# Two weight loads ahead of chunk 16, a choice that reads PSUM, and counts in front of the early products

## The chip, the cores and the metric

One core of one Trainium2 chip runs the whole program once. The time is device microseconds of that core, from the start of the program to its end; lower is better. Five engines work at once, each through its own instruction list in order: TensorE (PE in the profile; its weight loads are PEld), VectorE (DVE), ScalarE (ACT), GpSimd (POOL) and SyncE (SP, which issues most of the transfers). An instruction starts when it is the next one on its engine and the semaphores it waits for have been raised by others.

## The reference, cut to what matters

A gated recurrence over 4 batches, 8 heads, 768 positions and 48 dimensions is followed by a layer of 16 experts (4 groups of 4), of which each of the 3072 rows of 384 numbers uses the one that two argmaxes pick.

```python
for t in range(S):
    state = alpha[:, :, t, :, None] * state + einsum('bhd,bhe->bhde', k[:, :, t], v[:, :, t])
    y[:, :, t] = einsum('bhd,bhde->bhe', q[:, :, t], state)
x = y.transpose(0, 2, 1, 3).reshape(3072, 384)

g_logits = x @ w_group
g_idx = argmax(g_logits, axis=1)
for g in range(4):
    xg = x[g_idx == g]
    e_logits = xg @ w_expert[g]
    e_idx = argmax(e_logits, axis=1)
    for e in range(4):
        h = maximum(xg[e_idx == e] @ w1[g, e], 0.0)
        out[rows of (g, e)] = (g_w * e_w)[:, None] * (h @ w2[g, e])
```

g_w and e_w are the softmax values of the picked group and expert; w1 is 384 x 1024 and w2 is 1024 x 384 for each expert. Everything is float32.

## The kernel before, in words

**First part, the recurrence.** The 3072 positions are 24 chunks of 128, six to a batch, numbered 0 to 23. For a chunk, DVE scans the decays backwards (L449, `rev`), takes a reciprocal (L455, `turn`) and scans them forwards (L460, `forth`); POOL multiplies keys and queries with the results (L465, L469); PE makes the scores (L481, tile zs). They are masked in two halves, each either by DVE (L490, `mask`) or by an ACT copy (L495) and a POOL cut (L498); the list `BY_VECTOR` (L762) says for each chunk how many halves DVE takes. PE turns the keys (L510, `turn_k`), forms what the state gains (L523, `gain`), the chunk's own outputs (L547, `own_out`) and the outputs from the state (L556, `from`). DVE adds the gain to the state (L532, `grow`), ACT scales it in four pieces for the next chunk (L536, `scale`) and copies the outputs (L562, `copy`). From that copy PE makes the rows and logits (L569, `row`). PE's tile zo is shared: `turn_k` of chunk n waits for the `copy` of chunk n-2.

The six chunks of batches 0 to 2 are chosen for together (groups 0, 1, 2); batch 3 is cut into chunks 18 to 20, 21 and 22, and 23 (groups 3, 4, 5). DVE sums a group's logits (L589; L581 for the last three chunks) and picks the expert by a chain of small operations (L635 to L650, with the weights in L666 to L673). PE counts the rows of each expert (`counts`, c0 to c5: L743, L747, L751), DVE turns the counts into places (L696, L703), and POOL scatters each chunk's rows into slots in DRAM by an indirect transfer (L719). Eight fills with blank rows (L787) have to land before the first scatter.

**Weights and buffers.** Six `in` buffers hold the chunks' inputs. The two `w1` and two `w2` buffers of the expert weights hold chunks 6 and 8, and 7 and 9 (L428), before they hold weights. A load of chunk n from 16 on waits until chunk n-6 is through with its buffer. All of these transfers are issued by SP in one fixed order; L848 says before which chunk's load the two weights of expert 0 stand.

**What sets the order.** Every step of the first part is entered in a table with an engine, a guessed duration and its predecessors. A list scheduler (class Plan) turns the table into one order of instructions for each engine, and that order is fixed in the program. PE's steps and SP's steps keep the order in which they are entered. The guess for a transfer on SP is its bytes at 400 GB/s.

**End of the first part.** The list LAST (L764) orders PE behind `from` of chunk 22: counts of groups 3 to 5 (c3, c4, c5), rows of chunks 22 and 23, own outputs of chunk 23 (own, with `from` of chunk 23 behind them), and h0 to h7: the hidden products (L272, tile zs) of the first 96 rows of expert 0, whose rows were fetched after group 1. Their second products (L272 from early_hT) follow. Meanwhile the expert with the most rows after batch 2 is chosen on DVE (`choose_ahead`, L329 to L339), so that SP can load its weights; its rows are fetched (L771) as soon as chunk 23 has been scattered, transposed on DVE (L779, xt_ahead), and PE starts with it.

**Second part, the experts.** 16 jobs in turn, each 24 hidden and 24 result products for up to 216 rows, with weights loaded two jobs ahead; the results are transposed, weighted and scattered to the output.

Of the kernel before, what the change touches and what calls it, by code (L numbers as in the profile page):

```python
# [13 lines left out]
F32 = mybir.dt.float32  # L14
# [9 lines left out]
P = 128  # L24
# [3 lines left out]
class Plan:  # L28
# [6 lines left out]
    def add(self, name, eng, us, fn, after=(), row=None, lands=0.0, lead=0.0,  # L35
            rest=0.0):
        after = [a for a in after if a is not None]
        first = self.tail_of.get(row)
        if row is not None:
            after.append(first)  # L40
            self.tail_of[row] = name
        self.ops[name] = dict(eng=eng, us=us, fn=fn, after=after, lands=lands, first=first,
                              lead=lead, rest=rest)
        return name
# [66 lines left out]
def gla_then_hierarchical_moe(  # L111
# [34 lines left out]
    NT = in_d.shape[0]  # L146
# [13 lines left out]
    NE = w1_d.shape[0]  # L160
# [5 lines left out]
    FIXED, EARLY, CAPS = 1, (96,), (CAP,)  # L166
    EARLY_T, AHEAD_T = (B - 2) * NC, (B - 1) * NC
    NIN = 6
    NS = NE - FIXED
# [10 lines left out]
    cp = ctx.enter_context(tc.tile_pool(name="consts", bufs=1))  # L180
# [68 lines left out]
    def load_w1(i, e):  # L249
        w1 = wp.tile([P, DC, F], F32, name="w1")  # L250
        weights[i] = [w1]
        return nc.sync.dma_start(out=w1.rearrange("p c f -> p (c f)"),
                                 in_=w1_d[ds(e, 1)].rearrange("o p f -> p (o f)")).ins

    def load_w2(i, e):
        w2 = wp.tile([P, FC, DM], F32, name="w2")
        weights[i].append(w2)
        nc.sync.dma_start(out=w2.rearrange("p c f -> p (c f)"),
                          in_=w2_d[ds(e, 1)].rearrange("o p f -> p (o f)"))
# [56 lines left out]
    ahead = jobs[FIXED]  # L316
# [2 lines left out]
    is_ahead = cp.tile([P, NS], F32, name="is_ahead")  # L319
    ahead_i = cp.tile([P, 1], I32, name="ahead_i")  # L320

    def keys_of(t, key):
        cnt = cp.tile([P, NE], F32, name=f"cnt{t}")
        nc.vector.tensor_tensor(out=cnt, in0=seen[:, t, :], in1=seen[:, 0, :], op=ALU.subtract)
        nc.vector.scalar_tensor_tensor(out=key, in0=cnt[:, FIXED:NE], scalar=float(NE),
                                       in1=tile_f[:, FIXED:NE], op0=ALU.mult, op1=ALU.subtract)
        return cnt

    def choose_ahead():  # L329

        key = cp.tile([P, NS], F32, name="key_ahead")
        keys_of(AHEAD_T, key)
        most = cp.tile([P, 1], F32, name="most")
        nc.vector.tensor_reduce(out=most, in_=key, axis=AX.X, op=ALU.max)
        nc.vector.tensor_tensor(out=is_ahead, in0=key, in1=most.to_broadcast([P, NS]),
                                op=ALU.is_equal)
        nc.vector.tensor_tensor(out=key, in0=is_ahead, in1=tile_f[:, FIXED:NE], op=ALU.mult)
        with nc.allow_low_precision("whole numbers below 2**24"):
            nc.vector.tensor_reduce(out=ahead_i, in_=key, axis=AX.X, op=ALU.add)  # L339

    def ahead_on(eng):
        return nc.values_load(ahead_i[0:1, 0:1], engines=[eng], min_val=FIXED, max_val=NE - 1,
                              skip_runtime_bounds_check_because="an index of one of NE")

    def by_number():
        key = cp.tile([P, NS], F32, name="key")
        cnt = keys_of(NT, key)
        nc.vector.scalar_tensor_tensor(out=key, in0=is_ahead, scalar=float(2 * NE * N), in1=key,
                                       op0=ALU.mult, op1=ALU.add)
        sq = cp.tile([P, NS, NS], F32, name="sq")  # L350
        nc.vector.tensor_tensor(out=sq, in0=key[:, None, :].to_broadcast([P, NS, NS]),
                                in1=key[:, :, None].to_broadcast([P, NS, NS]), op=ALU.is_gt)
        rank = cp.tile([P, NS], F32, name="rank")
        nc.vector.tensor_reduce(out=rank, in_=sq, axis=AX.X, op=ALU.add)
        nc.vector.tensor_tensor(out=sq, in0=tile_f[:, 0:NS, None].to_broadcast([P, NS, NS]),
                                in1=rank[:, None, :].to_broadcast([P, NS, NS]), op=ALU.is_equal)
        nc.vector.tensor_tensor(out=sq, in0=sq, in1=tile_f[:, None, FIXED:NE]
                                .to_broadcast([P, NS, NS]), op=ALU.mult)
        order = cp.tile([P, NS], I32, name="order")
        with nc.allow_low_precision("whole numbers below 2**24"):  # L360
            nc.vector.tensor_reduce(out=order, in_=sq, axis=AX.X, op=ALU.add)
        return cnt, rank, order
# [4 lines left out]
    PE, DVE, ACT, POOL, SP = ENG.PE, ENG.DVE, ENG.Activation, ENG.Pool, ENG.SP  # L367
    made = {}

    with ExitStack() as gla:  # L370
# [8 lines left out]
        starts, gates = both[:, 0:HP * A1], both[:, 512:1024]  # L379
        at = HP * A1 - 512  # L380
# [3 lines left out]
        for i in range(2):  # L384
# [3 lines left out]
                at += k  # L388
            scratch.append(m)
        desc, floor = gates[:, at:at + 4], gates[:, at + 4:at + 4 + FIXED]  # L390
        state = [buf.tile([R, HP, 64], F32, name=f"state{i}") for i in range(2)]

        def warm(n):
# [365 lines left out]
        LEAD = 3.6  # L759
        REST, LATE = 0.7, 18  # L760
        WARM = (38, 5)
        BY_VECTOR = [1, 1, 0, 1, 1, 2, 1, 0, 0, 0, 1, 2, 0, 0, 1, 0, 1, 2, 2, 1, 0, 2, 1, 0]  # L762
        COUNTED = [15, 19, 11]
        LAST = 'c3 row22 own h0 c4 row23 h1 h2 h3 c5 h4 h5 h6 h7'.split()  # L764
        groups = [(b, c0, c1) for b in range(B) for c0, c1 in zip(cuts[b], cuts[b][1:])]

        def fetch_fixed(job, eng, j0, j1):
# [24 lines left out]
        add = plan.add  # L792
# [23 lines left out]
        def dma(name, us, fn, bytes_, after=(), lands=2.0):  # L816
            add(name, SP, max(us, bytes_ / L / 1e3), fn, after=list(after), row="sp", lands=lands)
# [24 lines left out]
        def before_load(k, item):  # L842
            order.insert(order.index(("load", k)), item)

        before_load(4, ("wr", 0))
        for i, k in enumerate((8, 9, 10, 11, 12, 13, 14, 14)):
            before_load(k, ("fill", i))
        for k, item in ((18, ("w1", 0)), (20, ("w2", 0))):  # L848
            before_load(k, item)
        for kind, n in order:  # L850
            if kind == "load":
# [60 lines left out]
        def VECTOR(n):  # L912
            return BY_VECTOR[n]

# [66 lines left out]
        def add_counts(g):  # L981
            b, c0, c1 = groups[g]
            t0 = b * NC + c0
            PEQ(f"counts{g}", 0.35 + 0.07 * (c1 - c0), partial(counts, g, b, c0, c1),
                after=[made["chosen", g], late(t0 - 1, "count"), late(t0 - 1, "floor")],
                reader=f"own{g}")
            also[f"own{g}"] = f"count{b * NC + c1 - 1}"
            add_send(g, b, c0, c1, f"counts{g}", made["weighed", g],
                     [f"kept_r{t}" for t in range(b * NC + c0, b * NC + c1)])
            if b * NC + c1 == EARLY_T:  # L990
                for e in range(FIXED):
                    add_fixed(e, EARLY_T, 4)
            if b * NC + c1 == AHEAD_T:
                add_ahead(g)
# [11 lines left out]
                after=[f"fetch{j}", f"fetch_{j}"])  # L1006

        def add_ahead(g):
            add("ahead", DVE, 1.1, choose_ahead,
                after=[f"count{AHEAD_T - 1}", f"place{g}", made["weighed", g]], lead=8.0)  # L1010

            def by_sp():
                ahead["e"] = ahead_on(SP)

            def by_act():
                ahead["e_act"] = ahead_on(ACT)

            add("ahead_s", SP, 0.8, by_sp, after=["ahead"], row="sp")
            add("ahead_a", ACT, 0.7, by_act, after=["ahead"])
            dma("w11", 0.45, lambda: load_w1(1, ahead["e"]), 1.57e6)  # L1020
            dma("w21", 0.45, lambda: load_w2(1, ahead["e"]), 1.57e6)
# [73 lines left out]
        early_ring = []  # L1095
        for item in LAST:
            if item == "own":
# [10 lines left out]
        plan.ops[f"xt{FIXED}"]["lead"] = 11.0  # L1108
        numbered = []
        add("number", DVE, 2.5, lambda: numbered.extend(by_number()), after=[f"count{NT - 1}", "ahead"])  # L1110
        plan.emit(patience=0.4, seed=10, spread=0.0)

# [182 lines left out]
    cnt, rank, order = numbered  # L1295
# [4 lines left out]
    for j, job in enumerate(jobs):  # L1300
# [6 lines left out]
        w1, w2 = weights.pop(j)  # L1307
# [16 lines left out]
    with tc.For_i(0, n_left, iteration_sync="staggered") as i:  # L1324
# [7 lines left out]
        w1, w2 = weights.pop("left")  # L1332
# [83 lines left out]
```

## Time and profile before

| | |
|---|---|
| time, median of 3 runs | 396.46 us (395.11 to 397.73) |
| the profiled execution | 396.02 us, of which 394.3 us are the span of the profile |
| TensorE busy / weight loads | 96% / 91% of the span |
| GpSimd / VectorE / ScalarE busy | 51% / 40% / 30% |
| first part | 0 to 139.0 us |
| experts | 139.0 to 382.9 us, the rest delivers the last results |
| moved by DMA | 98.35 MB |

Times inside the profile count from the start of the span. A row of the timeline gives the start, the time from the start of its first instruction to the end of its last, the engine, the line, the operation with the tiles that it writes and reads, how many instructions are merged, and in brackets how long the engine had been idle before and what ended that. A row of the windows gives for a stretch the busy time of each engine with the number of instructions, the granted share of TensorE's clock (1.00 is 2.4 GHz, 0.50 is 1.2 GHz), the mean share of the 16 DMA engines that was busy, and GB/s.

### The profile page before, as it was taken

The page shows a single profiled execution, that of the slowest core. Times are in us where ns is not written, and L with a number is a line of the kernel's source. Part 1 is how long each engine was busy: PE and PEld are TensorE (multiplying, and loading weights), DVE is VectorE, ACT ScalarE, POOL GpSimd, SP SyncE. Part 2 cuts the span into 40 slices and gives each one's busy share as a digit, 9 for nine tenths or more (in the row PEclk, how much of TensorE's full clock was granted, in tenths as well). Part 3 has the DMA queues.
Part 4 walks back from the last instruction along what each step waited for, and adds up shares of the span by engine and source line. Part 5 has one row for each costly group of instructions (what it writes and reads, how often), then busy time and mean ns, then how long its engine had stood idle before and what let it go on. Part 6 is the DMA issues. An engine that isn't in the chain of part 4 may idle for free.

```text
span 394.3 us, 8690 instructions
## 1 busy us (share of the span) xinstructions
PE 377.9 (96%) x3381; PEld 360.3 (91%) x3381; DVE 157.5 (40%) x342; ACT 119.4 (30%) x312; POOL 202.5 (51%) x236
## 2 busy tenths in 40 slices
PE   7999999989988889999999999999999999999993
PEld 5888888878877889999999999999999999999993
DVE  7799988688965320211472022020220220220110
ACT  1676766655663111202112121211111211211120
POOL 4988869978966020516153261542632523523543
PEclk9999999989999989999999999999999999999998
DMA  8999987987366497758586586865876877775500
GB/s 286 390 414 408 408 332 253 412 316 258 138 243 264 106 358 216 220 183 269 226 267 204 188 241 236 281 210 194 275 256 214 252 266 243 227 279 213 186 16 31
DMA packets 30954, 98.35 MB, mean 249 GB/s; under 512 B 18005, under 2 KB 18387, under 8 KB 26560
## 3 DMA queue, kind: packets, MB, share of 16 engines
q1 hardware_dynamic: 24880, 86.88, 63.0%
q0 software_dynamic: 4832, 9.55, 7.0%
q10 hardware_dynamic: 1200, 1.36, 1.1%
q8 instruction: 27, 0.44, 0.4%
q14 instruction: 15, 0.12, 0.1%
HBM read 82.61 MB, written 15.60 MB: 249 GB/s over the span
## 4 chain that ended last, share of the span: by engine, by line
PE 78%; DMA 15%; issue 2%; POOL 2%; ACT 1%; SPq 0%; DVE 0%; POOLq 0%; ACTq 0%; DVEq 0%
PE bank L272 62%; DMA in<-in_rows_dram 8%; DMA slots_d<-blank 4%; PE bank L569 3%; DMA w<-in_rows_dram 3%; PE zs L272 3%; PE zo L547 3%; PE zs L481 2%; PE zo L556 2%; PE bank L523 1%; PE zo L510 1%; ACT yt L562 1%; POOL out_dram L1148 1%; PE bank L751 0%; SPq L443 0%
## 5 line engine op out<-in xcount | busy, mean ns | idle before, releaser
L1148 POOL DMA_INDIRECT out_dram<-yq,dst_q x101 | 98.3, 973 | 158.1 <-DVE yq L1144 109.3
L272 PE MATMUL bank<-hT,w 128*128 128x216 f32 (+14 forms) x720 | 120.8, 328 | 0.0
L272 PEld LDWEIGHTS bank<-hT,w 128*128 128x128 f32 x720 | 118.7, 190 | 0.0
L272 PE MATMUL bank<-xt_e,w 128*128 128x213 f32 (+14 forms) x720 | 117.4, 323 | 0.0
L272 PEld LDWEIGHTS bank<-xt_e,w 128*128 128x128 f32 x720 | 115.4, 190 | 0.0
L1165 DVE CAST dst_q<-xq 128x7 int32<-128x7 f32 (+1 forms) x14 | 2.4, 172 | 160.1 <-DMA out_dram<-yq,dst_q 160.1
L287 ACT ACTIVATE hT<-bank 128x432 f32<-128x432 f32 (+15 forms) x64 | 31.3, 489 | 98.4 <-PE bank L272 71.6
L303 ACT COPY yT<-bank 128x432 f32<-128x432 f32 (+29 forms) x30 | 12.1, 403 | 104.3 <-PE bank L272 104.3
L719 POOL DMA_INDIRECT slots_d<-xr,place x24 | 24.2, 1008 | 11.8 <-DMA in<-in_rows_dram 3.5
L569 PE MATMUL bank<-wr,yt 112*128 112x116 f32 x192 | 26.7, 283 | 3.3 <-ACT yt L562 3.3
L569 PEld LDWEIGHTS bank<-wr,yt 112*128 112x128 f32 x192 | 23.9, 196 | 4.1 <-ACT yt L562 3.9
L449 DVE TENSOR_TENSOR_SCAN kd<-in,starts 112x516 f32<-112x516 f32 x20 | 24.4, 1222 | 7.1 <-DMA in<-in_rows_dram 6.6
L465 POOL TENSOR_TENSOR in<-in,kd 112x512 f32<-112x512 f32 x20 | 23.6, 1181 | 6.3 <-DVE kd L449 6.2
L460 DVE TENSOR_TENSOR_SCAN cq<-in,starts 112x516 f32<-112x516 f32 x20 | 24.5, 1227 | 2.0 <-POOL in L469 0.6
L469 POOL TENSOR_TENSOR in<-in,cq 112x512 f32<-112x512 f32 x20 | 23.6, 1182 | 3.0 <-DMA in<-in_rows_dram 1.2
L1141 DVE STREAM_TRANSPOSE yq<-yT 128x672 f32<-128x672 f32 (+2 forms) x16 | 12.9, 808 | 28.6 <-ACT yT L303 28.5
L481 PE MATMUL zs<-in 48*128 48x128 f32 x320 | 23.2, 284 | 1.0 <-POOL in L469 0.9
L547 PE MATMUL zo<-sm,in 128*48 128x128 f32 (+1 forms) x320 | 23.5, 280 | 0.2
L481 PEld LDWEIGHTS zs<-in 48*128 48x128 f32 x320 | 19.4, 187 | 4.4 <-issue 2.4
L536 ACT ACTIVATE state<-sums,kd 112x48 f32<-112x48 f32 x64 | 18.3, 330 | 8.7 <-DVE sums L532 8.7
L547 PEld LDWEIGHTS zo<-sm,in 128*48 128x48 f32 (+1 forms) x320 | 19.1, 133 | 1.1 <-POOL sm L498 0.4
L562 ACT COPY yt<-zo 112x512 f32<-112x512 f32 x24 | 14.1, 585 | 19.7 <-PE zo L556 14.0
(153 smaller groups left out, 349.6 us busy)
## 6 DMA issues: line engine op xcount, KB each, us to landing
w<-in_w_dram SPq DMA_DIRECT2D x34, 1536.0 KB
in<-in_rows_dram SPq DMA_DIRECT2D x17, 962.5 KB
slots_d<-blank SPq DMA_DIRECT2D x8, 686.0 KB
w<-in_rows_dram SPq DMA_DIRECT2D x4, 962.5 KB
xq<-slots_d SPq DMA_DIRECT2D x28, 85.8 KB
xq<-slots_d SPq DMA_DIRECT2D x28, 73.5 KB
out_dram<-yq,dst_q POOLq DMA_INDIRECT x101
in<-in_rows_dram SPq DMA_DIRECT2D x3, 258.5 KB
```

The costliest lines, as they stand in the source:

```text
L272: nc.tensor.matmul(z, lhsT=w, rhs=x, start=first, stop=last, skip_group_check=True)
L287: nc.scalar.activation(out=hT[:, f0:f0 + 2, 0:n], in_=z[:, 0:2 * n].rearrange("p (f t) -> p f t", f=2), func=AF.Relu)
L449: nc.vector.tensor_tensor_scan(out=flat(c.kd[:, p0:p1])[:, ::-1], data0=c.t[0:R, A1 * p1:A1 * p0:-1], data1=one_col.to_broadcast([R, A1 * ...
L460: nc.vector.tensor_tensor_scan(out=flat(c.cq[:, p0:p1]), data0=c.t[0:R, A1 * p0:A1 * p1], data1=starts[0:R, A1 * p0:A1 * p1], initial=1.0, ...
L465: nc.gpsimd.tensor_tensor(out=c.k[:, p0:p1], in0=c.k[:, p0:p1], in1=c.kd[:, p0:p1, 1:A1], op=ALU.mult)
L469: nc.gpsimd.tensor_tensor(out=c.q[:, p0:p1], in0=c.q[:, p0:p1], in1=c.cq[:, p0:p1, 1:A1], op=ALU.mult)
L481: nc.tensor.matmul(c.zs[i][:, p, :], lhsT=c.k[r, p, :], rhs=c.q[r, p, :], start=True, stop=True)
L536: nc.scalar.activation(out=c.st[:, p, 0:D], in_=chunks[c.n - 1].sums[:, p], func=AF.Copy, scale=c.kd[:, p, 0:1])
L547: nc.tensor.matmul(of(c.zo, p)[o], lhsT=c.v[:, h * D:h * D + o.stop - o.start], rhs=c.sm[:, i, p, :], start=(p < 2), stop=(c.bc == 0), ski ...
L569: nc.tensor.matmul(z[:, p * W:(p + 1) * W], lhsT=c.yt[:, p, :], rhs=wr[:, p, :], start=True, stop=True)
L719: sent = nc.gpsimd.indirect_dma_start(out=slots_by[t], out_offset=bass.IndirectOffsetOnAxis(ap=m["place"][:, c:c + 1], axis=0), in_=xr[:, ...
L1148: nc.gpsimd.indirect_dma_start(out=out_by.popleft().rearrange("n (j w) -> (n j) w", j=4), out_offset=bass.IndirectOffsetOnAxis(ap=dst[:, b ...
```

## The change

Three things are edited. The loads of w1 and w2 of expert 0 stand in front of chunk 16's load instead of in front of chunks 18 and 20. `choose_ahead` writes its counts and keys into the PSUM tile that also holds `starts` and the other small operands, instead of into SBUF. In LAST, h0 moves from between "own" and c4 to behind row23, and h3 from in front of c5 to behind it, so that two and a half pairs are left behind c5 instead of two. With these, `BY_VECTOR` changes for five chunks: DVE takes one half more of chunks 9, 13 and 23, and one less of chunks 16 and 22.

```diff
-    def keys_of(t, key):
-        cnt = cp.tile([P, NE], F32, name=f"cnt{t}")
+    def keys_of(t, key, cnt):
         nc.vector.tensor_tensor(out=cnt, in0=seen[:, t, :], in1=seen[:, 0, :], op=ALU.subtract)
         nc.vector.scalar_tensor_tensor(out=key, in0=cnt[:, FIXED:NE], scalar=float(NE),
                                        in1=tile_f[:, FIXED:NE], op0=ALU.mult, op1=ALU.subtract)
-        return cnt
-
-    def choose_ahead():
-
-        key = cp.tile([P, NS], F32, name="key_ahead")
-        keys_of(AHEAD_T, key)
+
+    def choose_ahead(cnt, key):
+
+        keys_of(AHEAD_T, key, cnt)
...
         desc, floor = gates[:, at:at + 4], gates[:, at + 4:at + 4 + FIXED]
+        at += 4 + FIXED
+        ahead_at = [gates[:, at:at + NE], gates[:, at + NE:at + NE + NS]]
...
-        BY_VECTOR = [1, 1, 0, 1, 1, 2, 1, 0, 0, 0, 1, 2, 0, 0, 1, 0, 1, 2, 2, 1, 0, 2, 1, 0]
+        BY_VECTOR = [1, 1, 0, 1, 1, 2, 1, 0, 0, 1, 1, 2, 0, 1, 1, 0, 0, 2, 2, 1, 0, 2, 0, 1]
         COUNTED = [15, 19, 11]
-        LAST = 'c3 row22 own h0 c4 row23 h1 h2 h3 c5 h4 h5 h6 h7'.split()
+        LAST = 'c3 row22 own c4 row23 h0 h1 h2 c5 h3 h4 h5 h6 h7'.split()
...
-        for k, item in ((18, ("w1", 0)), (20, ("w2", 0))):
+        for k, item in ((16, ("w1", 0)), (16, ("w2", 0))):
             before_load(k, item)
...
-            add("ahead", DVE, 1.1, choose_ahead,
+            add("ahead", DVE, 1.1, partial(choose_ahead, *ahead_at),
```

On SP, around the loads of chunks 14 to 23 (L443), this is a piece of the difference; L787 are the fills, L252 is w1 and L258 is w2 of expert 0, L771 the fetch of its rows:

```order
 L443 DMA in<-in_rows_dram 128x1925
 L787 DMA slots_d<-blank 112x2x784 x2
-L443 DMA in<-in_rows_dram 128x1925 x4
-L252 DMA w_1138<-in_w_dram 128x3072
 L443 DMA in<-in_rows_dram 128x1925 x2
-L258 DMA w_1284<-in_w_dram 128x3072
-L443 DMA in<-in_rows_dram 128x1925 x4
+L252 DMA w_857<-in_w_dram 128x3072
+L258 DMA w_927<-in_w_dram 128x3072
+L443 DMA in<-in_rows_dram 128x1925 x8
 L771 DMA rows_0_88<-slots_d 32x3x98 x4
```

The load of chunk 13, the fills, and the loads of chunks 14 and 15 are followed at once by both weights, and chunks 16 to 23 come behind them; before, chunks 16 and 17 came ahead of w1, and 18 and 19 ahead of w2.

On DVE, from the backward scan of chunk 16 (the first row; L490 is a mask, L589 to L642 the choice of group 1, L532 the state of chunk 13), before:

```order
L449 SCALAR_TENSOR_TENSOR kd<-in,starts 112x516
L455 RECIPROCAL starts<-kd 112x4
L460 SCALAR_TENSOR_TENSOR cq<-in,starts 112x516
L589 TENSOR_REDUCE lg<-lgp 128x120
L490 TENSOR_TENSOR sm<-zs_1153,causal 128x512
L635 TENSOR_REDUCE starts<-lg 128x30
L636 TENSOR_TENSOR dl<-lg,starts 128x120
L638 SCALAR_TENSOR_TENSOR oh<-dl,starts 128x120
L532 TENSOR_TENSOR sums<-state_117,bank 112x192
```

and in the changed kernel:

```order
L449 SCALAR_TENSOR_TENSOR kd<-in,starts 112x516
L490 TENSOR_TENSOR sm<-zs_1092,causal 128x512
L455 RECIPROCAL starts<-kd 112x4
L460 SCALAR_TENSOR_TENSOR cq<-in,starts 112x516
L589 TENSOR_REDUCE lg<-lgp 128x120
L635 TENSOR_REDUCE starts<-lg 128x30
L490 TENSOR_TENSOR sm<-zs_1155,causal 128x512
L636 TENSOR_TENSOR dl<-lg,starts 128x120
L638 SCALAR_TENSOR_TENSOR oh<-dl,starts 128x120
L642 TENSOR_REDUCE starts<-oh 128x30
L532 TENSOR_TENSOR sums<-state_117,bank 112x192
```

A mask of chunk 13 now stands directly behind the scan of chunk 16, and one more step of the choice stands in front of the state of chunk 13. ACT's order around that state is the same as before: three pieces of the scaling that read it (L536), then the copy of chunk 13 (L562).

On PE, behind the outputs from the state of chunk 23, the changed kernel has (L743 to L751 are counts, L569 the rows of chunk 23, L272 the early products):

```order
L743 MATMUL bank<-picked,before 128x32
L747 LDWEIGHTS ones
L747 MATMUL bank<-picked,ones 128x32
L747 LDWEIGHTS ones
L747 MATMUL bank<-picked,ones 128x16
L751 MATMUL bank<-seen,ident 128x48
L569 MATMUL bank<-wr,yt 128x116 x4
L272 MATMUL zs_2022<-xt_0_89,w_857 128x96 x6
L272 MATMUL zs_2043<-xt_0_89,w_857 128x96 x3
L743 MATMUL bank<-picked,before 128x16
```

Before, three of the L272 products stood ahead of the first of these rows, and nine stood between the rows of chunk 23 and the last counts, as now.

## Rows read from the trace of the kernel before

**Rows 1.** The page: busy time of the engines, and two lines of the list of transfers (count, and KB of each).

```profile
PE 377.9 (96%) x3381; PEld 360.3 (91%) x3381; DVE 157.5 (40%) x342; ACT 119.4 (30%) x312; POOL 202.5 (51%) x236
...
w<-in_w_dram SPq DMA_DIRECT2D x34, 1536.0 KB
in<-in_rows_dram SPq DMA_DIRECT2D x17, 962.5 KB
```

**Rows 2.** Windows of 5 us: the engines' busy time, then the granted clock, the DMA share and GB/s.

```profile
50.00:55.00 5.00, 5.00 (x85) 4.45 (x84) 4.07 (x9) 3.75 (x12) 1.55 (x3) 1.00 1.04 421
55.00:60.00 5.00, 4.55 (x80) 3.65 (x72) 4.30 (x7) 2.21 (x7) 4.77 (x5) 1.00 0.47 188
60.00:65.00 5.00, 5.00 (x80) 4.31 (x74) 4.08 (x6) 3.50 (x9) 4.81 (x6) 1.00 0.73 223
...
75.00:80.00 5.00, 3.65 (x69) 3.00 (x67) 2.71 (x7) 2.04 (x7) 4.82 (x6) 1.00 1.03 410
80.00:85.00 5.00, 4.77 (x53) 4.39 (x57) 3.74 (x7) 3.06 (x10) 3.46 (x4) 0.66 0.92 385
...
125.00:130.00 5.00, 4.59 (x42) 4.59 (x43) 3.10 (x21) 1.80 (x7) 2.63 (x5) 1.00 0.23 86
...
135.00:140.00 5.00, 2.89 (x21) 2.71 (x20) 1.88 (x7) 0.56 (x2) 0.00 (x0) 0.89 0.74 173
140.00:145.00 5.00, 5.00 (x23) 4.83 (x22) 0.97 (x2) 0.53 (x1) 2.90 (x3) 0.77 1.00 413
```

**Rows 3.** Timeline of SP's queue, the transfers issued behind the last fills: the loads of chunks 14 to 17 in one row, w1 of expert 0, the loads of chunks 18 and 19; the last row is the loads of chunks 16 and 17 by themselves, from a shorter stretch. Start and the time over which they were issued.

```profile
39.69 25.05 SPq L443 DMA_DIRECT2D in<-in_rows_dram  x4
64.80 0.42 SPq L252 DMA_DIRECT2D w<-in_w_dram  x1
68.63 5.02 SPq L443 DMA_DIRECT2D in<-in_rows_dram  x2
...
60.28 4.46 SPq L443 DMA_DIRECT2D in<-in_rows_dram  x2
```

**Rows 4.** Timeline of DVE from the backward scan of chunk 16 to the state of chunk 14.

```profile
65.44 1.23 DVE L449 TENSOR_TENSOR_SCAN kd<-in,starts 112x516 f32<-112x516 f32 x1 [0.61 <-DMA in<-in_rows_dram]
66.70 0.19 DVE L455 RECIPROCAL starts<-kd 112x4 f32<-112x4 f32 x1
66.99 1.23 DVE L460 TENSOR_TENSOR_SCAN cq<-in,starts 112x516 f32<-112x516 f32 x1
68.28 0.99 DVE L589 TENSOR_REDUCE lg<-lgp 128x120 f32<-128x480 f32 x1
69.52 0.69 DVE L490 TENSOR_TENSOR sm<-zs,causal 128x512 f32<-128x512 f32 x1 [0.26 <-PE zs L481]
70.13 0.27 DVE L635 TENSOR_REDUCE starts<-lg 128x30 f32<-128x120 f32 x1
70.44 0.28 DVE L636 TENSOR_TENSOR dl<-lg,starts 128x120 f32<-128x120 f32 x1
71.57 0.35 DVE L532 TENSOR_TENSOR sums<-state,bank 112x192 f32<-112x192 f32 x1 [0.54 <-PE bank L523]
...
77.80 1.23 DVE L449 TENSOR_TENSOR_SCAN kd<-in,starts 112x516 f32<-112x516 f32 x1 [2.19 <-DMA in<-in_rows_dram]
78.95 0.33 DVE L532 TENSOR_TENSOR sums<-state,bank 112x192 f32<-112x192 f32 x1
```

**Rows 5.** Timeline of ACT in the same stretch: scaling and copy of chunk 13 (first two rows) and of chunk 14 (last two).

```profile
71.96 0.78 ACT L536 ACTIVATE state<-sums,kd 112x48 f32<-112x48 f32 x3 [0.38 <-DVE sums L532]
73.34 0.59 ACT L562 COPY yt<-zo 112x512 f32<-112x512 f32 x1 [0.60 <-PE zo L556]
...
79.37 0.33 ACT L536 ACTIVATE state<-sums,kd 112x48 f32<-112x48 f32 x1 [2.96 <-DVE sums L532]
79.61 0.57 ACT L562 COPY yt<-zo 112x512 f32<-112x512 f32 x1
```

**Rows 6.** Timeline of PE in the same stretch: the turned keys of chunk 15 and those of chunk 16.

```profile
73.98 0.60 PE L510 MATMUL zo<-ident,in 112*128 112x112 f32 x4
...
80.23 0.60 PE L510 MATMUL zo<-ident,in 112*128 112x112 f32 x4 [1.58 <-ACT yt L562]
```

**Rows 7.** Timeline of all engines at the choice of the picked expert.

```profile
108.83 1.60 DVE L335 TENSOR_TENSOR is_ahead<-key_ahead,most 128x15 f32<-128x15 f32 x1
109.20 1.19 POOL L469 TENSOR_TENSOR in<-in,cq 112x512 f32<-112x512 f32 x1
...
112.42 0.35 DVE L532 TENSOR_TENSOR sums<-state,bank 112x192 f32<-112x192 f32 x1 [0.59 <-ACT sm L495]
```

**Rows 8.** Timeline of PE from the end of the outputs of chunk 23 (h0, the rows of chunk 23, the last early hidden products) to the first product of the picked expert; a product of the order above is two instructions here; the last two rows are ACT's copy of chunk 23 and the scatter that POOL issues just before it.

```profile
122.82 0.91 PE L272 MATMUL zs<-xt,w 128*128 128x96 f32 x6
125.41 1.15 PE L569 MATMUL bank<-wr,yt 112*128 112x116 f32 x8 [1.37 <-ACT yt L562]
128.67 2.90 PE L272 MATMUL zs<-xt,w 128*128 128x96 f32 x24
139.03 3.22 PE L272 MATMUL bank<-xt_ahead,w 128*128 128x216 f32 x8 [2.11 <-issue]
...
124.77 0.59 ACT L562 COPY yt<-zo 112x512 f32<-112x512 f32 x1 [2.25 <-PE bank L751]
...
122.94 0.98 POOL L719 DMA_INDIRECT slots_d<-xr,place  x1 [0.30 <-issue]
```

More of the change, by code (lines that the diff above doesn't have):

```diff
@@ L346, in by_number @@
         key = cp.tile([P, NS], F32, name="key")
-        cnt = keys_of(NT, key)
+        cnt = cp.tile([P, NE], F32, name="cnt")
+        keys_of(NT, key, cnt)
         nc.vector.scalar_tensor_tensor(out=key, in0=is_ahead, scalar=float(2 * NE * N), in1=key,
```

## The prediction, made before the changed kernel ran

> **What bounds the kernel now.** I read the list of busy times first: TensorE is busy 96% of the time [rows 1], so a change can win little more than its pauses, and the time that it spends at a lower clock behind them. Next the windows of 5 us, to find where that is. Two places are within reach of this change. In the stretch 75 to 85 us PE misses 1.35 us of the first window, and the granted clock of the second is 0.66 [rows 2]; at 135 to 145 us it misses 2.1 us and the clock is 0.89 and then 0.77. Then the timelines of single engines, followed backwards from each pause. The first pause is 1.58 us in front of the turned keys of chunk 16, which wait for ACT's copy of chunk 14 [rows 6]. The copy stands behind a scaling that waited for DVE [rows 5], and DVE had stood 2.19 us waiting for the load of chunk 18 before it could add up the state [rows 4]. That load was issued at 68.63, right behind w1 of expert 0 at 64.80 [rows 3], on a DMA that was full then (share 1.03, 410 GB/s [rows 2]). So the weights, put where they are, cost a pause of 1.58 us. With the clock lost, 5.00 x (1 - 0.66) = 1.70 us, that makes **3.28 us**. The second pause, 2.11 us, is the wait for the rows of the picked expert [rows 8]; the clock behind it costs 0.55 + 1.15 = 1.70 us more.
>
> **The weights ahead of chunk 16.** Removed: the late load of chunk 18, 3.28 us. It now has only the loads of chunks 16 and 17 ahead of it in the queue.
>
> Moved onto the load of chunk 16: it was issued at 60.28 [rows 3] when DMA was half idle, and DVE waited only 0.61 us for it, until 65.44 [rows 4]. Now both weights, 2 x 1536 KB = 3.15 MB [rows 1], stand in front. They can't begin before the loads of chunks 14 and 15 are through, since DMA is full to 55 us (share 1.04 [rows 2]). From 55 to 65 us, at 410 GB/s, 4.10 MB can be moved, and 188 x 5 us + 223 x 5 us = 2.06 MB are moved already, chunk 16 among them. That leaves room for 2.04 MB; the other 1.11 MB take 2.7 us. I put the landing of chunk 16 at 65.44 + 2.7 = **68.1 us**. Bounds: 65.4 (nothing is delayed) and 70.9 (as much again, see the second rival).
>
> What waits for it: on DVE, behind the backward scan of chunk 16, now stand (order above, durations of [rows 4]) the scan 1.23, a mask 0.69, reciprocal 0.19, scan 1.23, logits 0.99, reduction 0.27, mask 0.69 and three small steps of 0.28 each, 6.13 us, with 0.2 of gaps 6.33. Before, the state of chunk 13 was added 71.57 - 65.44 = 6.13 us behind the scan; a half more of masks and one more small step have taken the place of 0.26 and 0.54 us of waiting. So that addition comes at 68.1 + 6.33 = 74.4 instead of 71.57. ACT starts its three scalings 0.39 later, they take 0.78, and the copy of chunk 13 takes 0.59 [rows 5]: it ends at 76.2, and PE's turned keys of chunk 15, at 73.98 before without a pause [rows 6], wait until 76.3. That is a **new pause of 2.3 us**. After pauses of 1.58 and 2.11 us the clock fell, for 1.70 us each time, and after 1.37 us it stayed (125 to 130 us at 1.00 [rows 2, 8]); so I add 1.70. New cost 4.0, removed 3.28: **+0.7 us**. The load of chunk 18, two loads of 0.99 MB behind chunk 16, lands 2 x 2.4 us after it, at about 73. DVE was ready for it at 77.80 - 2.19 = 75.6 [rows 4], and now 2.9 later. That wait is gone.
>
> One rule bears on the delay. The load of chunk 18 was issued 3.8 us behind w1 and landed 9.2 us after its issue, against 5.2 for chunk 16, which had no weights in front [rows 3, 4]. The Trainium skill ("DMA: Bandwidth & Descriptors", section "Queues, rings and completion order") says that on each DMA engine what one queue holds is started in the order in which it was put there; by that rule chunk 16 stands behind all of both weights, as in my sum. The trace agrees, with 9.2 against 5.2 us. Were the rate shared between transfers instead, chunk 16 would hardly be later than before, and the sum would be that of the first rival.
>
> **The choice in PSUM.** One of its steps took 1.60 us while POOL multiplied queries in SBUF from 109.20 to 110.39 [rows 7]. If the change takes all of that waiting away, DVE gains up to 1.3 us there (1.60 less the 0.28 of such a step [rows 4]). But behind it DVE stands idle 0.59 us at 112.42, waiting for others [rows 7], and no pause of PE follows. I take 0; the bounds are -0.6 and, if an operand in PSUM is slower, +0.3.
>
> **The end.** Four units of early hidden products, 24 instructions, took 2.90 us, so one of six instructions takes 0.72 [rows 8]. Moving h0 behind row23 takes 0.72 of cover from the pause there: it grows from 1.37 to 2.09, as long as ACT's copy of chunk 23 starts at 124.77 again. The copy is not held by PE: the outputs it reads were done by 122.82, but POOL was issuing a scatter from 122.94 to 123.92, and nothing in the change removes that. The last counts come no earlier, with h0 in h3's place in front of them. Moving h3 behind them shortens the last pause by 0.72, to 1.39. So the two pauses change places: 2.09 is about the length after which the clock fell, 1.39 about that after which it didn't. So 1.70 us go at the end, and up to 1.70 come in front of the last counts, on which the picked expert's rows hang. **Net 0**; bounds -1.7 (the clock stays at both) and +1.7 (it falls at both). The masks moved between DVE and POOL are in the DVE sum above for chunk 13; the others I price at nothing, under DVE's 40% and POOL's 51% of busy time [rows 1]. Where that cover is gone, a half costs DVE 0.69.
>
> **Sum.** +0.7 + 0 + 0. The profiled execution took 396.02, so **396.7 us**. The median of the runs is 396.46, 0.44 above it, within their spread.
>
> **Rivals.**
> *Faster: the load of chunk 16 lands before 67.2.* For it: the queue may hold less in front than my windows say, since these mean a rate over 5 us and a part of what they count was small scatters that fit between. Against: the 0.94 MB of 55 to 60 us are 2.3 us of full DMA, and 7.7 for the weights and 2.4 for chunk 16 behind 57.3 make 67.4 with nothing between them. Then the pause at chunk 15's keys is at most 76.3 - 73.98 - 0.9 = 1.4, and the clock stays as after 1.37: -3.28 + 1.4 = -1.9, and up to -3.0 if it lands at 65.5. With the clock also kept at the end (-1.7) it is -3.6 to -4.7. That gives 391.3 to 394.1, as a point **392.8**.
>
> *Slower: chunk 16 is as late against its bytes as chunk 18 was.* Behind chunk 16's landing stood, up to that of chunk 18, the loads of chunks 17 and 18, 0.99 MB each, w1 with 1.57 MB [rows 1], and some scatters, 0.4 MB by my estimate: 3.95 MB, 9.6 us at 410 GB/s from 65.4, so 75.0; it landed at 77.8 [rows 4], 2.8 later. With that, chunk 16 lands at 70.9, the pause is 5.1 and the first part costs 5.1 + 1.7 - 3.28 = +3.5: **399.5**. From a landing at 67.4 on, the change costs more than it removes (pause 1.6 and clock 1.70 against 3.28); slower by 1% only from 71.8. Against it: between 55 and 65 us fewer other transfers were under way, 188 and 223 GB/s.
>
> *The copy of chunk 23 is no longer held.* DVE takes a half of chunk 23's masks from POOL, so the scatter may fall elsewhere. The copy could start at about 123.0 instead of 124.77; everything behind would be 1.8 earlier, the pauses shorter: -1.8 to -3.5, with the first part's +0.7 **394.2**. Against: POOL's scatter was ready and waited for issue alone (0.30 [rows 8]).
>
> **How the numbers follow.** About 1%, 4 us, is what a measurement of this kernel can tell from no change; so faster is below 392.5 and slower above 400.4. Chances: forecast 0.54, first rival 0.27, second 0.12, third 0.07. Of the first some 0.15, of the third 0.02 and of the forecast's low end 0.01 lie below 392.5: faster 0.18. Of the second 0.05 and of the forecast with +1.7 at the end and a later load 0.02 lie above 400.4: slower 0.07. Same 0.75. The forecast's own range is 395 to 398.4 (the end's bounds of 1.7 either way); to hold 8 in 10 it has to reach into both rivals: **392.2 to 399.6**.
>
> **What would show it.** On DVE a wait for DMA of some 3 us in front of the backward scan of chunk 16, and none for chunk 18. On PE a pause of about 2.3 us in front of the turned keys of chunk 15, released by ACT, with the clock below 1 in the window behind it, and none in front of those of chunk 16. The choice's step near 0.3 us without an effect on PE. In front of the rows of chunk 23 a pause near 2.1, and a last one near 1.4 with a clock of 1.00 behind it. A landing of chunk 16 before 67 us would prove the first term wrong, and a last counts row later than 128.4 plus the first part's shift by more than 1.7 would prove the end wrong.

## The result, and the profile after

The changed kernel took 397.52 us in the median of 20 executions, against 394.61 for 20 of the kernel before: a ratio of **1.0097** (95% interval 1.0068 to 1.0125), some 3.8 us more. The ratios here and below leave out executions more than 1.5% above the fastest of their kernel, one of 981.59 us of the changed kernel among them; by the medians of all executions it is 2.9 us. The time lies in the forecast's range and the ratio under its bound of 1%, though the interval reaches beyond; either figure is more than the +0.7 of its sum. The profiled execution took 397.13 (span 395.3).

The windows of 5 us of the changed kernel, to set beside [rows 2] (columns as there):

```profile
55.00:60.00 5.00, 4.19 (x74) 3.55 (x72) 4.19 (x6) 2.39 (x9) 3.97 (x4) 1.00 1.02 422
60.00:65.00 5.00, 5.00 (x78) 4.28 (x74) 4.53 (x7) 3.51 (x10) 4.93 (x5) 1.00 1.01 422
65.00:70.00 5.00, 4.70 (x78) 4.02 (x76) 0.92 (x1) 3.15 (x10) 4.81 (x7) 1.00 1.01 413
70.00:75.00 5.00, 2.71 (x25) 2.59 (x26) 4.44 (x7) 1.39 (x5) 3.13 (x3) 0.85 0.89 340
75.00:80.00 5.00, 5.00 (x74) 4.33 (x73) 3.80 (x11) 2.93 (x9) 2.79 (x3) 0.81 0.25 64
80.00:85.00 5.00, 5.00 (x82) 4.42 (x81) 3.58 (x5) 3.54 (x11) 4.30 (x5) 1.00 0.62 207
...
125.00:130.00 5.00, 3.09 (x20) 2.97 (x21) 2.13 (x14) 1.30 (x4) 3.21 (x5) 0.81 0.42 158
130.00:135.00 5.00, 5.00 (x41) 5.00 (x41) 3.34 (x17) 1.23 (x5) 0.98 (x1) 0.85 0.14 51
...
140.00:145.00 5.00, 4.67 (x30) 4.51 (x30) 2.85 (x8) 0.77 (x2) 1.17 (x2) 1.00 0.96 302
```

DMA is now full to 70 us, where it was half idle; the bad window of 80 to 85 us is gone, and in its place stands 70 to 80 us: 2.29 us of PE missing and a clock of 0.85 and 0.81, 0.75 + 0.95 = 1.70 us. At the end the low clock has moved from 135 to 145 us to 125 to 135 us.

DVE's timeline (scan of chunk 16, the mask half of chunk 13, the state of chunk 13, scan of chunk 18), beside [rows 4]:

```profile
70.42 1.23 DVE L449 TENSOR_TENSOR_SCAN kd<-in,starts 112x516 f32<-112x516 f32 x1 [4.51 <-ACT yt L562]
71.57 0.67 DVE L490 TENSOR_TENSOR sm<-zs,causal 128x512 f32<-128x512 f32 x1
...
77.17 0.36 DVE L532 TENSOR_TENSOR sums<-state,bank 112x192 f32<-112x192 f32 x1 [0.92 <-PE bank L523]
...
80.80 1.20 DVE L449 TENSOR_TENSOR_SCAN kd<-in,starts 112x516 f32<-112x516 f32 x1
```

and PE's (scores of chunk 14 in the kernel before, then in the changed one; turned keys of chunk 15; then the end: counts, rows of chunk 23, early products, the same 18 early products in the kernel before, first product of the picked expert), beside [rows 6, 8]:

```profile
68.26 1.16 PE L481 MATMUL zs<-in 48*128 48x128 f32 x16
...
72.29 1.16 PE L481 MATMUL zs<-in 48*128 48x128 f32 x16 [2.59 <-DVE sm L490]
...
79.55 0.60 PE L510 MATMUL zo<-ident,in 112*128 112x112 f32 x4
...
125.22 0.19 PE L743 MATMUL bank<-picked,before 128*128 128x32 bf16 x1 [0.31 <-DVE picked L650]
...
127.40 1.43 PE L569 MATMUL bank<-wr,yt 112*128 112x116 f32 x8 [1.69 <-ACT yt L562]
128.63 3.55 PE L272 MATMUL zs<-xt,w 128*128 128x96 f32 x18
...
126.40 2.16 PE L272 MATMUL zs<-xt,w 128*128 128x96 f32 x18
...
141.54 4.65 PE L272 MATMUL bank<-xt_ahead,w 128*128 128x216 f32 x24 [0.33 <-ACT yT L303]
```

The scan of chunk 18 no longer waits, but the scan of chunk 16 waited 4.51 us. (ACT's copy that the row names ended at the moment when the load landed; in the second profile below the same wait is put down to the load.) PE's pause of 2.59 us is in front of the scores of chunk 14, earlier than forecast: they wait for the mask half of chunk 13, which DVE does right behind that scan. Before, they ran at 68.26 without a pause. The turned keys of chunk 15 then find all they need. In front of the rows of chunk 23 there is 0.31 + 1.69 = 2.00 us of pause (forecast 2.09); the last one is 0.33 instead of 1.39. PE comes to it later, as the 18 instructions between took 3.55 us at the low clock instead of 2.16, but that isn't all: in the run with all halves back, below, they took 2.16 and the last pause is 0.33 too. The picked expert's rows also came sooner behind the issue of their fetch: DVE began to transpose them 4.0 us behind it (136.52 to 140.53), against 5.5 before (132.59 to 138.05). Why isn't shown.

The choice in PSUM, DVE's timeline beside [rows 7] (the step behind the one of 1.60 in the kernel before, then the two steps in the changed one):

```profile
110.47 0.17 DVE L337 TENSOR_TENSOR key_ahead<-is_ahead,tile_f 128x15 f32<-128x15 f32 x1
...
111.03 0.17 DVE L332 TENSOR_TENSOR is_ahead<-starts,most 128x15 f32<-128x15 f32 x1
111.23 1.39 DVE L334 TENSOR_TENSOR starts<-is_ahead,tile_f 128x15 f32<-128x15 f32 x1
```

The step that took 1.60 takes 0.17, and the next takes 1.39 instead of 0.17. POOL's product ran from 111.39 to 112.57 as recorded; the step of 0.17 began 0.36 us ahead of it, as the one of 1.60 had (0.37: 108.83 and 109.20). The wait went to the step that still has both operands in SBUF. The Trainium skill ("SBUF — State Buffer", section "Who interferes with whom") says that a DVE instruction with two inputs in SBUF contends with a GpSimd instruction that reads SBUF, and that one with at most one such input, outside the modes that use two ports, doesn't; the trace agrees, 0.17 against 1.39 us.

### The profile page after: what moved, and what is told of

The parts are those of the page before. It is cut to its first block, busy times and chain, and to the rows that moved or that the text cites. A ratio compares the mean times of both kernels' runs of the same rounds, so it can differ in the third digit from the quotient of the medians.

```text
span 395.3 us, 8690 instructions
## 1 busy us (share of the span) xinstructions
PE 377.6 (96%) x3381; PEld 360.3 (91%) x3381; DVE 157.0 (40%) x343; ACT 119.3 (30%) x311; POOL 201.7 (51%) x235
## 4 chain that ended last, share of the span: by engine, by line
PE 89%; DMA 4%; issue 2%; DVE 1%; POOL 1%; ACT 1%; SPq 0%; POOLq 0%; ACTq 0%; DVEq 0%
PE bank L272 61%; PE bank L569 5%; PE zo L547 5%; PE zs L481 5%; DMA in<-in_rows_dram 4%; PE zo L556 3%; PE zs L272 3%; PE bank L523 2%; PE zo L510 2%; PE bank L751 1%; POOL out_dram L1148 1%; DVE kd L449 1%; ACT yt L562 1%; SPq L443 0%; POOL out_dram L1291 0%
## 5 line engine op out<-in xcount | busy, mean ns | idle before, releaser
L272 PE MATMUL bank<-hT,w 128*128 128x216 f32 (+14 forms) x720 | 120.8, 328 | 0.0
L272 PEld LDWEIGHTS bank<-hT,w 128*128 128x128 f32 x720 | 118.7, 190 | 0.0
L272 PE MATMUL bank<-xt_e,w 128*128 128x213 f32 (+14 forms) x720 | 117.4, 323 | 0.0
L272 PEld LDWEIGHTS bank<-xt_e,w 128*128 128x128 f32 x720 | 115.4, 190 | 0.0
L569 PE MATMUL bank<-wr,yt 112*128 112x116 f32 x192 | 27.1, 286 | 3.9 <-ACT yt L562 3.1
L569 PEld LDWEIGHTS bank<-wr,yt 112*128 112x128 f32 x192 | 24.3, 199 | 4.8 <-ACT yt L562 3.6
L547 PE MATMUL zo<-sm,in 128*64 128x128 f32 (+1 forms) x320 | 22.9, 276 | 0.2 <-ACT kt L515 0.2
L498 POOL TENSOR_SCALAR_AFFINE_SELECT sm<-sm 128x512 f32<-128x512 f32 x27 | 16.9, 635 | 7.2 <-ACT sm L495 7.1
L536 ACT ACTIVATE state<-sums,kd 112x48 f32<-112x48 f32 x64 | 17.9, 329 | 7.2 <-DVE sums L532 6.7
L562 ACT COPY yt<-zo 112x512 f32<-112x512 f32 x24 | 14.1, 587 | 19.2 <-PE zo L556 12.7
```

Of the source, the lines that this page charges most:

```text
L272: nc.tensor.matmul(z, lhsT=w, rhs=x, start=first, stop=last, skip_group_check=True)
L547: nc.tensor.matmul(of(c.zo, p)[o], lhsT=c.v[:, h * D:h * D + o.stop - o.start], rhs=c.sm[:, i, p, :], start=(p < 2), stop=(c.bc == 0), ski ...
L562: nc.scalar.copy(out=c.yt.rearrange("r (a b) s -> r b a s", b=2), in_=c.zo[0:R, :, 0:2 * P].rearrange("r b (a s) -> r b a s", a=2))
L569: nc.tensor.matmul(z[:, p * W:(p + 1) * W], lhsT=c.yt[:, p, :], rhs=wr[:, p, :], start=True, stop=True)
```

## The experiments

Ratios are against executions of the kernel before on the same chip, with 95% intervals.

**The kernel before, again.** No edit.

> The kernel before, unchanged: it measures how far two profiled executions of one kernel lie apart, and how often its two pauses and the falls of the clock behind them come. If the pause in front of chunk 16's turned keys (1.58 us in the first profile) is there in each execution, it is again above 1.3 us and the clock in 80 to 85 us below 0.8; if it was an accident of that execution, it is under 0.8 us and the clock stays at 1.00, and then the weights had nothing to remove. Ratio 1.000 within 0.003.

1.0027 (0.9992 to 1.0063). PE's timeline (turned keys of chunk 16; first product of the picked expert) and windows:

```profile
80.89 0.60 PE L510 MATMUL zo<-ident,in 112*128 112x112 f32 x4 [1.84 <-ACT yt L562]
...
138.35 7.90 PE L272 MATMUL bank<-xt_ahead,w 128*128 128x216 f32 x42 [2.04 <-issue]
```
```profile
80.00:85.00 5.00, 4.11 (x48) 3.67 (x52) 4.54 (x11) 3.69 (x11) 3.87 (x5) 0.76 0.94 392
85.00:90.00 5.00, 5.00 (x80) 4.33 (x80) 3.51 (x8) 1.90 (x7) 3.26 (x3) 0.90 0.66 226
135.00:140.00 5.00, 2.96 (x21) 2.83 (x21) 2.56 (x8) 0.24 (x1) 0.00 (x0) 1.00 0.82 204
140.00:145.00 5.00, 5.00 (x29) 5.00 (x28) 0.29 (x1) 1.06 (x2) 2.91 (x3) 1.00 1.02 416
```

The pause behind the late chunk 18 is there again, 1.84 us and 1.20 + 0.50 = 1.70 us of clock. The last pause is 2.04, but this time the clock stayed at 1.00 behind it. The span is 392.1, 2.2 us under the first profile's, of which 1.70 is that clock. The execution on which the forecast was built was a long one of its kernel.

**The weights alone.**

```diff
-        for k, item in ((18, ("w1", 0)), (20, ("w2", 0))):
+        for k, item in ((16, ("w1", 0)), (16, ("w2", 0))):
```

> The kernel before with only the two weight loads moved ahead of chunk 16's load. Theory A (the loss comes from the weights: chunk 16 lands some 11 us behind chunk 15, PE pauses 2 to 3 us for it, clock lost 1.7 us): +1 to +3 us, ratio 1.003 to 1.008, with a DVE wait of over 3 us for chunk 16. Theory B (the loss comes from the order at the end and the halves of masks): ratio within 0.002 of 1.000.

1.0000 (0.9963 to 1.0037; medians of all executions 393.41 and 395.04), as theory B said; theory A's lower end is inside, its middle isn't. DVE's scan of chunk 16 and its mask half of chunk 14, and PE's scores of chunk 14, scores of chunk 15 and turned keys of chunk 15:

```profile
69.10 1.23 DVE L449 TENSOR_TENSOR_SCAN kd<-in,starts 112x516 f32<-112x516 f32 x1 [4.60 <-ACT yt L562]
...
72.65 0.71 DVE L490 TENSOR_TENSOR sm<-zs,causal 128x512 f32<-128x512 f32 x1
```
```profile
67.94 1.16 PE L481 MATMUL zs<-in 48*128 48x128 f32 x16
...
73.46 1.25 PE L481 MATMUL zs<-in 48*128 48x128 f32 x16 [0.73 <-POOL sm L498]
75.79 0.60 PE L510 MATMUL zo<-ident,in 112*128 112x112 f32 x4 [1.07 <-ACT yt L562]
```

Chunk 16 is as late as in the changed kernel (a wait of 4.60), but here ACT and POOL make both halves of chunk 13, and the scores of chunk 14 don't wait at all. Those of chunk 15 wait 0.73, until DVE's half of chunk 14 is done, which stands behind the late scan as well (the row names POOL, whose last step ended at 73.22, ahead of DVE's at 73.36). The keys wait 1.07, and the clock stayed at 1.00 from 70 to 80 us. So the late load by itself costs no more than the punctual chunk 18 wins.

**The weights back.** The same edit reversed in the changed kernel.

> The changed kernel with the two weight loads put back ahead of chunks 18 and 20; choice in PSUM, order at the end and halves stay. Theory A: the DVE wait for chunk 16 is under 1 us, the one for chunk 18 is back with 1 to 2 us, and the time is that of before, ratio 0.997 to 1.003. Theory B: the pause before the rows of chunk 23 stays near 1.7 to 2.1 us with the clock behind it at 0.8, and the ratio stays at 1.005 to 1.010.

0.9994 (0.9951 to 1.0037), as theory A said. Misses: chunk 16's scan waited 2.17 us instead of under 1, and the pause before the rows of chunk 23 was 1.68 with the clock at 0.71 behind it, as B expected, without costing the kernel anything that can be measured.

**Neither alone, both together.** The halves (and the other two edits) with the old place of the weights: nothing. The new place with everything else as before: nothing. The loss needs both, so two runs gave the halves back in the changed kernel, all of them, and that of chunk 13 alone:

```diff
-        BY_VECTOR = [1, 1, 0, 1, 1, 2, 1, 0, 0, 1, 1, 2, 0, 1, 1, 0, 0, 2, 2, 1, 0, 2, 0, 1]
+        BY_VECTOR = [1, 1, 0, 1, 1, 2, 1, 0, 0, 0, 1, 2, 0, 0, 1, 0, 1, 2, 2, 1, 0, 2, 1, 0]
```
```diff
-        BY_VECTOR = [1, 1, 0, 1, 1, 2, 1, 0, 0, 1, 1, 2, 0, 1, 1, 0, 0, 2, 2, 1, 0, 2, 0, 1]
+        BY_VECTOR = [1, 1, 0, 1, 1, 2, 1, 0, 0, 1, 1, 2, 0, 0, 1, 0, 0, 2, 2, 1, 0, 2, 0, 1]
```

> The changed kernel with the halves of the masks as before (weights ahead of chunk 16, choice in PSUM and order at the end stay). Theory A1 (the loss is the mask half of chunk 13, which DVE now does behind the late scan of chunk 16, while PE's scores of chunk 14 wait for it): no pause above 1.2 us in front of the scores of chunk 14 and no clock below 1.00 at 70 to 80 us, as in the run with the weights alone; 2 to 4 us less than the changed kernel, ratio 0.998 to 1.004 against before. Theory A2 (the loss is the order at the end): the pause before the rows of chunk 23 is 1.9 to 2.1 us with the clock fallen behind it, and the ratio stays at 1.006 or more.

> The changed kernel with one half of chunk 13 alone given back to ACT and POOL. Theory A1: the same gain as with all halves back, 2 to 4 us less than the changed kernel, ratio 0.998 to 1.004. If another half (of chunks 9, 16, 22 or 23) is the cause, the pause at 72 us is gone or not, but the ratio stays at 1.006 or more.

All halves back: 1.0039 (0.9996 to 1.0082; medians 396.95 and 396.64). The scores of chunk 14 don't wait; as with the weights alone, the pauses are at the scores of chunk 15 (0.92) and at its keys (1.03). The clock fell there all the same (0.70 from 75 to 80 us), which A1 hadn't expected. Before the rows of chunk 23 the pause was 1.78 without a fall, which speaks against A2. Chunk 13 alone: 1.0043 (0.9969 to 1.0118), too wide to tell 0 from the whole loss, and the medians (400.60 and 396.64) speak for the loss. Its profile has no pause at the scores of chunk 14, as A1 says, but one of 1.08 us with a fall of the clock at the keys of chunk 15 and one of 2.17 before the rows of chunk 23. That half makes the pause at the scores of chunk 14; that it makes the whole loss isn't shown.

**The order at the end alone.**

```diff
-        LAST = 'c3 row22 own h0 c4 row23 h1 h2 h3 c5 h4 h5 h6 h7'.split()
+        LAST = 'c3 row22 own c4 row23 h0 h1 h2 c5 h3 h4 h5 h6 h7'.split()
```

> The kernel before with the changed order at the end alone. Theory A2: the pause before the rows of chunk 23 grows from 1.3 to 2.0 us and the clock falls there (1.7 us), the last pause shrinks to 1.3 or less; since the clock behind the last pause fell in only one of the four executions that have it, the end loses 1 to 1.7 us: ratio 1.002 to 1.005. The forecast's view (two pauses change places, net 0): ratio 0.998 to 1.002.

0.9997 (0.9951 to 1.0042): the forecast's net 0 holds, within 1.9 us either way. In its profile the pause is 1.82, and the clock fell further than ever behind it:

```profile
120.00:125.00 5.00, 2.88 (x33) 2.43 (x29) 1.87 (x12) 0.90 (x3) 3.08 (x6) 0.81 0.47 179
125.00:130.00 5.00, 5.00 (x26) 4.99 (x26) 2.25 (x14) 1.20 (x4) 0.93 (x2) 0.50 0.20 76
130.00:135.00 5.00, 5.00 (x33) 5.00 (x32) 2.71 (x10) 0.70 (x3) 0.98 (x1) 0.66 0.19 59
```

**The changed kernel again, and with the order at the end back** (the edit above reversed).

> The changed kernel, unchanged: whether its loss and its pauses repeat. Theory C (the weights and the new halves cost together what neither costs alone: DVE does a mask half of chunk 13 behind the late scan of chunk 16, and POOL does two scatters in a row while it waits for the fills): a pause of 2 to 3 us in front of the scores of chunk 14 with the clock fallen behind it, a pause of about 1 us near 58 us, ratio 1.005 to 1.011. If the first 60 us, which lay 1.2 us behind in the first profile, were an accident of that execution, they lie within 0.5 us of the others here, and the ratio is 1.003 to 1.008.

> The changed kernel with the order at the end as before; weights ahead of chunk 16, halves and choice in PSUM stay. Theory C: the pauses in front of the scores of chunk 14 stays, the one before the rows of chunk 23 shrinks from 1.7 to about 1.0 us without a fall of the clock, the last pause is back with 2 us: 0 to 1 us less than the changed kernel on the same chip. If the order at the end were the cause of the loss, 2 to 3.5 us less and a ratio of 0.999 to 1.003.

Again: **1.0114** (1.0061 to 1.0166). The loss repeats (2.9 us by the medians, as in the result). PE's lag of 1.2 us up to 60 us in the first profile doesn't, nor does its pause of 0.81 near 58 us; but pauses of 0.73 and 1.32 stand there in the profiles with the order at the end back and with chunk 13's half back, so it is something that comes and goes, and why isn't shown. DVE, then PE, then the windows:

```profile
69.53 1.23 DVE L449 TENSOR_TENSOR_SCAN kd<-in,starts 112x516 f32<-112x516 f32 x1 [5.18 <-DMA in<-in_rows_dram]
70.68 0.67 DVE L490 TENSOR_TENSOR sm<-zs,causal 128x512 f32<-128x512 f32 x1
```
```profile
71.40 2.08 PE L481 MATMUL zs<-in 48*128 48x128 f32 x16 [3.96 <-DVE sm L490]
```
```profile
70.00:75.00 5.00, 3.60 (x24) 3.38 (x25) 4.83 (x9) 0.49 (x2) 2.19 (x2) 0.50 0.69 277
75.00:80.00 5.00, 5.00 (x74) 4.28 (x74) 2.93 (x9) 2.95 (x10) 2.79 (x3) 0.82 0.15 46
```

The pause is 3.96 us here, since nothing had held PE up before it, and the clock cost 2.50 + 0.90 = 3.40. Against the second profile of before that is 7.36 for 3.54; that kernel had a pause of 0.88 at 59 us besides, which leaves +2.9. PE comes to the rows of chunk 23 at 127.44 against 124.81, and to the picked expert at 142.02 against 138.35. So of 3.7 us, 2.6 came before the rows of chunk 23 and 1.0 behind them.

With the old order at the end: 1.0056 (1.0010 to 1.0101). The scores wait 2.62 us again, but this time without a fall (clock 1.00 from 70 to 80 us), and PE comes to the picked expert at 138.25. Two things came otherwise than expected: the clock fell behind the pause before the rows of chunk 23, though that was only 1.31 us, and the last pause is 0.48 instead of 2.

```profile
124.63 1.36 PE L569 MATMUL bank<-wr,yt 112*128 112x116 f32 x8 [1.31 <-ACT yt L562]
```
```profile
125.00:130.00 5.00, 5.00 (x33) 5.00 (x33) 2.31 (x14) 1.48 (x5) 2.09 (x4) 0.66 0.41 158
```

The time is 0.6% less than the changed kernel, with intervals that overlap: what the order at the end costs on top isn't settled between nothing and some 2 us.

**The weights behind chunk 23**, in the kernel before, in the changed kernel, and in the changed kernel with the old order at the end:

```diff
-        for k, item in ((18, ("w1", 0)), (20, ("w2", 0))):
-            before_load(k, item)
+        order += [("w1", 0), ("w2", 0)]
```

> The kernel before with the two weight loads behind the load of chunk 23, where DMA was 0.24 to 0.32 busy at 100 to 110 us. Theory A: neither chunk 16 nor chunk 18 is late, no pause above 1 us and no fall of the clock before 110 us, 3.3 us less in an execution like the first profile: ratio 0.990 to 0.995. Theory B: the weights' place is worth nothing: ratio 0.998 to 1.002. Against both: expert 0's first products at 122 us would have to wait for w1, which is then seen as a pause with a DMA behind it.

> The changed kernel with the weights behind the load of chunk 23. Theory A1: neither chunk 16 nor chunk 18 is late, so the new halves find DVE in time and no pause above 1 us comes before 110 us; if the order at the end is harmless, the ratio equals that of the kernel before with the weights there (0.994); by theory A2 it is 1 to 1.7 us worse, 0.996 to 0.999.

> The changed kernel with the weights behind the load of chunk 23 and the order at the end as before; halves and choice in PSUM stay. Theory C: no late chunk, so the new halves cost nothing and may win some tenths; no pause above 1.2 us and no fall of the clock before the last pause: 0.987 to 0.994, better than both kernels. If the halves alone were the loss, 1.000 or more.

Before: **0.9936** (0.9885 to 0.9987), faster than both kernels, and by about 2.5 us than the kernel before, where 3.3 were expected. The scan of chunk 18 waits 0.43 us, PE has no pause above 0.4 us from 12 to 106 us, and no product of expert 0 waits for its weights. Changed: 0.9978 (0.9943 to 1.0014), between the two theories' figures, with 1.75 us before the rows of chunk 23 and a clock of 0.73 behind them. Old order at the end: 0.9979 (0.9946 to 1.0011), short of the expected 0.994 at most. In its profile chunk 16 is late again:

```profile
67.69 1.23 DVE L449 TENSOR_TENSOR_SCAN kd<-in,starts 112x516 f32<-112x516 f32 x1 [3.42 <-ACT state L536]
```
```profile
69.55 1.16 PE L481 MATMUL zs<-in 48*128 48x128 f32 x16 [1.46 <-DVE sm L490]
```

The load of chunk 16 landed some 2 us later than in the first of these three, with no weights ahead of it: by the trace's records of its arrival, 15 of its 16 parts were there by 65.5 us and the last at 67.6. The mask half behind its scan passed that straight on to PE. By the medians of all executions the three win alike (2.7, 2.8 and 2.4 us: 392.34 against 395.04, 393.80 against 396.64, 391.85 against 394.29), so whether the halves and the order at the end cost anything there isn't settled.

**The choice in PSUM alone**, by undoing the other edits.

> The kernel before with the choice in PSUM alone. The step that took 1.60 us takes 0.17, but the next step with two operands in SBUF takes over what is left of the wait, some 1.4 us, if POOL is still at its product; no pause of PE follows in either case: ratio 0.998 to 1.002. Were the choice on the path, up to 1.3 us less, 0.997.

0.9990 (0.9951 to 1.0030), and the wait is in the next step:

```profile
109.03 1.37 DVE L334 TENSOR_TENSOR starts<-is_ahead,tile_f 128x15 f32<-128x15 f32 x1
```

## Why the prediction was right, and where it wasn't

- **The load of chunk 18, 3.28 us removed: right.** The pause was no accident (1.58, 1.84, and 2.14 us in the run with the choice alone, each with a fall behind it; 1.32 without one in the run with the order at the end alone) and is gone; with the weights at the end of the queue some 2.5 us were won.
- **The landing of chunk 16 at 68.1: 1.0 to 1.4 us too early.** Where the start didn't lag, its scan began at 69.10 and 69.53. Behind 65 us the forecast gave the whole 410 GB/s to SP's queue. From 58.3 to 69.5 us of the second profile after, the list of DMA queues shows how the time was shared (packets, MB, share of the 16 engines):

```profile
q1 hardware_dynamic: 462, 4.00, 85.1%
q0 software_dynamic: 208, 0.67, 14.9%
```

  SP's queue moved 4.00 MB in 11.2 us, 357 GB/s; POOL's scatters had the rest. Besides, a load is through when its last part is: by the trace's records of its arrival, the parts of this one came from 67.5 to 69.4 us, those of the same load in the first profile of before from 64.9 to 65.3. How much of the lateness each of the two makes isn't shown.
- **What waits for it: the step that failed.** The forecast put the mask half of chunk 13 into DVE's sum, 0.69 us in front of the state of chunk 13, and let PE wait at the keys of chunk 15. It didn't ask who waits for the half itself: PE's scores of chunk 14. They lie before all of that in PE's order, so the pause comes earlier, 2.59, 3.96 and 2.62 us in three executions, where 2.3 were forecast. With the clock it cost 4.3, 7.4 and 2.6 against 4.0. The sum for the keys was also short by its own rows: between the scalings and the copy of chunk 13 ACT had waited 0.60 us for PE's outputs from the state [rows 5], which it leaves out.
- **The clock: a rule too simple.** The forecast let it fall behind pauses of 1.6 us and more, once, for 1.70. It fell behind one of 1.31 us and stayed behind one of 2.62 (last section), and it cost twice as much in the second profile after.
- **The end: one length right, the balance not shown.** The pause before the rows of chunk 23 is 2.00 for 2.09; the last one is 0.33 and 0.77 in the two profiles instead of 1.39. And the 1.70 credited for the last pause is mostly not there to be won: of the five other profiled executions with the old order and a last pause of 2.04 to 2.29 us, one (the choice alone) has the low clock behind it, four have 1.00. In its place the low clock now stands ahead of the last counts, on the way to the picked expert's rows: from the rows of chunk 23 to the first of its products it is 141.54 - 127.40 = 14.14 us (14.58 in the second profile), against 13.62 [rows 8] and 13.54. The time of the run with this edit alone allows 0 as well as 1 us.
- **The choice in PSUM, 0: right**; the wait moved on by one step.
- **The rivals.** The first needed chunk 16 by 67.2 and is refuted. The second, chunk 16 at 70.9, had the landing too late by as much as the forecast had it too early, but its +3.5 is near what the kernel lost (2.9 or 3.8 us), by another wait than its own. The third didn't come: the pause before the rows of chunk 23 stayed. What holds ACT's copy there isn't shown: the row names PE's counts and not POOL's scatter [rows 8], on which both the forecast and this rival rest.
- **The sum.** 396.7 was 0.8 under the measured 397.5, closer than its steps deserve: it stood on an execution 1.4 us above the median that 20 executions gave, which made up for part of a loss of 2.9, by the medians, that it had at 0.7. That it came so close is luck.

## What to carry to other kernels

When a late transfer is priced, list everything that stands behind the first instruction that waits for it on its engine, and for each of these who waits for it: a small step slipped in right behind the wait can hold up a bottleneck engine sooner than the chain that one has in mind. Look at two profiled executions before crediting a gain that rests on the clock. A long transfer that is needed late belongs behind the transfers that are needed soon, and changes that are each harmless have to be run together.

## What the runs showed of the hardware beyond that

The granted clock doesn't follow from the length of a pause. Behind a last pause of 2.11 it fell in the first profile of before (0.89, 0.77 [rows 2]) and stayed at 1.00 behind 2.04 in the second and behind 2.11 with the weights alone; before the rows of chunk 23 it fell behind 1.31 with the order at the end back and stayed behind 1.78 with all halves back; behind 2.62 us at the scores of chunk 14 it stayed, behind 2.59 and 3.96 it fell; behind 0.92 and 1.03 it fell, behind 0.73 and 1.07 it stayed. Each fall costs some 1.7 us, in three cases 3.4 and more, so single executions of one kernel lie several us apart (390.4 to 398.3 us in the 20 of before).
